# First query tiles of all batches computed ahead of everything else, in two units of 256 rows: a chunk-selecting attention with a feed-forward layer on one core

## The chip, the cores and the metric

The kernel runs on one core of a Trainium2 chip. Its time is the device time of one execution in microseconds (us); several executions are timed, and the median is compared. One further execution is profiled: its span runs from the first to the last instruction that the profiler saw on the core. The engines are PE (TensorE: matrix products and transposes), DVE (VectorE), ACT (ScalarE), POOL (GpSimd) and SP (SyncE, which only issues DMAs here). Each engine takes its instructions in order, and waits on semaphores for the others.

## What is computed

Attention over 4 batches, 8 heads, 768 positions and 64 channels, with a choice of key chunks per query; then a layer norm and a feed-forward layer with a residual:

```python
chunk = 32; nc = S // chunk; top_k = 6           # S = 768: 24 chunks
k_min, k_max = k_chunks.min(3), k_chunks.max(3)
ub = sum(maximum(q * k_min, q * k_max), -1)      # one bound per query and chunk
ub = where(pos // chunk >= chunk_index, ub, -1e9)
top_chunks = argsort(ub)[..., -top_k:]
scores = scale * q @ k.T                         # kept where chosen and causal
attn = softmax(where(sel & causal, scores, -1e9))
x = (attn @ v) heads side by side                # 4 x 768 x 512
xn = (x - mean) / sqrt(var + 1e-6) * g_ln
out = x + relu(xn @ w_ch1) @ w_ch2               # 512 -> 2048 -> 512
```

A query in the first 128 positions has at most four chunks in reach, which is fewer than six: it keeps all of them, and only the causal mask matters for it.

## The kernel before

Two heads of one batch form a pair; there are 16 pairs, numbered so that pairs 0 to 3 are batch 0, 4 to 7 batch 1, and so on. The 768 positions are six tiles of 128. The heads of a pair lie on the two halves of the 128 partitions.

**Loading.** `ldb` brings K or Q of a pair, 768 positions, in runs of 32 floats by four DMAs of SP, so that DVE's 32x32 block transpose (`turn`, L229) puts channels on partitions. Batch 0 is loaded differently (`ld`, runs of 64 floats, three tiles at a time) and is transposed by PE in float32 (L236). `ldv` brings V through POOL's queue, cast to half precision; `w1` and `w2` bring the two weight matrices through the same queue in four parts each, each behind a one-element copy that makes it wait for a pair's `kc`.

**Selection.** `kbound` (L288, L289) takes minimum and maximum of K per chunk; `kdiag` (POOL, L308 to L316) lays them out as operands. For pairs 4 to 15, `qhi` (L251 or L253), `qlo` (L256) and `qrel` (L262, L263) make half-precision parts of Q, `bounds` (L325) is 20 matmuls that give the bounds of tiles 1 to 5, and `select` adds the causal part (L351, L352), finds the eight largest of each row (L356) and compares (L357). For pairs 0 to 3 the same is done in float32 for half a sequence at a time (`qpos` on ACT, L338 on PE). The choice is transposed on PE (`maskt`, L366) and copied by DVE (`mring`) beside Q, so that masked scores come out of one matmul with 128 rows of contraction: 64 channels, and 24 rows of large negative numbers for chunks that were not chosen (`rrows`, from `RT`).

**Scores, values.** `smm(g, r, i)` (L419) fills one two-bank PSUM tile with up to four blocks of 128x128 per head; `sexp` (L427) takes the exponential on ACT, `diag` (L434) masks the diagonal blocks on POOL, `values` (L450) multiplies by V with a column of ones, `norm` (L464, L465) divides on DVE. r is 0 for query tiles 0 to 2, and 1 for tiles 3 to 5: six blocks and fifteen.

**Layer norm and feed-forward.** A unit is one half (b, r) of a batch, 384 rows; there are eight. `pstat` (L480) takes statistics per pair, `centre` (L489, L492) subtracts the mean and multiplies by the gain, `xt` (L509) is a transposing DMA of SP for each 128 rows, `m1` (L518) multiplies by two of the 16 column blocks of the first weight matrix into one PSUM tile, `relu` (L530 on ACT, L528 on DVE) writes half precision, `m2` (L543) adds four of 16 parts of the second product, and `fin` (L552, L557) scales, adds the residual and stores.

**Fillers.** `warm` and `busy` (L378, L117) are matmuls whose results nobody reads; they stand among the steps of batch 0.

**Order.** The text `ORDER` lists all steps; the loop under it calls them one after the other, and ties each instruction behind the one before it on the same engine. So every engine's queue is exactly that text, read from left to right. A number behind an @ selects another engine for a copy, or a number of fillers. What holds a step back is its data, and the buffers: PSUM has two two-bank tiles (`ps_m`: scores and first product) and four one-bank tiles (`ps_t`).

Of the kernel before, what the change touches and what calls it, by code (L numbers as in the profile page):

```python
# [19 lines left out]
def kernel(  # L20
# [10 lines left out]
    nc = tc.nc  # L31
# [8 lines left out]
    TR = NT // NR  # L40
# [19 lines left out]
    vap = ctx.enter_context(tc.tile_pool(name="vap", bufs=5))  # L60
# [3 lines left out]
    xp = ctx.enter_context(tc.tile_pool(name="xp", bufs=5))  # L64
    xcp = ctx.enter_context(tc.tile_pool(name="xcp", bufs=2))
    htp = ctx.enter_context(tc.tile_pool(name="htp", bufs=2))
# [8 lines left out]
    ident_b = const.tile([P, P], BF16, name="ident_b", tag="ident_b")  # L75
    causb = const.tile([P, NT - 1, 2, NCH], BF16, name="causb", tag="causb")
    causf = const.tile([P, NT - 1, 2, NCH], F32, name="causf", tag="causf")
    RT = const.tile([P, S], F16, name="RT", tag="RT")
    tiny = const.tile([1, 1], F32, name="tiny", tag="tiny")
    hsel = const.tile([P, 3, 2], F32, name="hsel", tag="hsel")  # L80
    mhalf = const.tile([P, TR], F32, name="mhalf", tag="mhalf")
    NK = 4
    QA = [ring.tile([P, S], F16, name=f"QA{i}", tag=f"QA{i}") for i in range(NK)]
    QB = [ring.tile([P, S], F16, name=f"QB{i}", tag=f"QB{i}") for i in range(NK)]
    KA = [ring.tile([P, S], F16, name=f"KA{i}", tag=f"KA{i}") for i in range(NK)]
    KB = [ring.tile([P, S], F16, name=f"KB{i}", tag=f"KB{i}") for i in range(NK)]
# [4 lines left out]
    MN = [ring.tile([P, NT - 1, P], F16, name=f"MN{i}", tag=f"MN{i}") for i in range(NM)]  # L91
# [7 lines left out]
    st = [dict() for _ in range(NG)]  # L99
    hf = {}  # L100
    x_tiles = {}

    other = [0]
    fill = {P: (8, 16, 32), 240: (4, 8, 16), 122: (8, 16, 32)}
# [7 lines left out]
    def busy(o):  # L114
        w = o.shape[1]
        for _ in range((0, *fill[w])[other[0]]):
            nc.tensor.matmul(o, ident_b, causb.rearrange("p s h c -> p (s h c)")[:, 0:w], start=True, stop=True)  # L117

    def consts():
        make_identity(nc, ident_f)
        rr = RT[0:64, :]
        nc.gpsimd.memset(rr, -NEGM)
        nc.gpsimd.affine_select(
            out=rr, in_=rr, compare_op=ALU.is_ge, fill=0.0,
            base=0, pattern=[[1, S]], channel_multiplier=-CH,
        )
        nc.gpsimd.affine_select(
            out=rr, in_=rr, compare_op=ALU.is_ge, fill=0.0,  # L130
            base=CH - 1, pattern=[[-1, S]], channel_multiplier=CH,
        )
        nc.gpsimd.memset(causb, 0.0)
        nc.gpsimd.affine_select(
            out=causb, in_=causb, compare_op=ALU.is_ge, fill=CAUSAL,
            base=P, pattern=[[P, NT - 1], [0, 2], [-CH, NCH]], channel_multiplier=1,
        )
        nc.vector.memset(hsel, 0.0)
        nc.scalar.activation(tiny, hsel[0:1, 0, 0:1], ACTF.Exp)
        nc.vector.memset(hsel[0:64, 0, 1:2], -KS)  # L140
        nc.vector.memset(hsel[64:P, 0, 0:1], -KS)
        nc.vector.memset(hsel[0:64, 1:3, 1:2], KS)
        nc.vector.memset(hsel[64:P, 1:3, 0:1], KS)
        for i in range(NM):
            nc.vector.memset(MN[i], 0.0)
        nc.vector.tensor_copy(ident_b, ident_f)
        nc.vector.tensor_copy(ident_h, ident_f)
        nc.scalar.dma_start(gall, moe_g_ln.rearrange("(o n) -> o n", o=1).to_broadcast([P, DM]))

    def late():  # L150
        nc.gpsimd.memset(mhalf, -0.5)
        nc.gpsimd.memset(causf, 0.0)
        nc.gpsimd.affine_select(
            out=causf, in_=causf, compare_op=ALU.is_ge, fill=CAUSAL,
            base=P, pattern=[[P, NT - 1], [0, 2], [-CH, NCH]], channel_multiplier=1,
        )

    def rinit(i):
        nc.vector.memset(QA[i][64:P, 0:P], 0.0)
        nc.vector.memset(QB[i][0:64, 0:P], 0.0)  # L160

    def rrows(i, r):
        c = slice(r * TR * P, (r + 1) * TR * P)
        eng = pick(nc.vector, nc.scalar)
        copy(eng, KA[i][64:P, c], RT[0:64, c])
        copy(eng, KB[i][0:64, c], RT[0:64, c])
# [3 lines left out]
    def w1(j, g):  # L170
        c = slice(j * HID // 4, (j + 1) * HID // 4)
        nc.gpsimd.tensor_copy(w1b[0:1, 0, c.start:c.start + 1], st[g]["kc"][0:1, 0, 0:1])
        nc.gpsimd.dma_start(w1b[:, :, c], w1_r[:, :, c])

    def w2(j, g):
        nc.gpsimd.tensor_copy(w2b[0:1, 4 * j, 0:1], st[g]["kc"][0:1, 0, NCH // 2:NCH // 2 + 1])
        nc.gpsimd.dma_start(w2b[:, 4 * j:4 * j + 4, :], w2_r[:, 4 * j:4 * j + 4, :])

    def ld(g, i):
        b, hp = divmod(g, HP)  # L180
        both = ldp.tile([P, 2, TR, 2, D], F32, name="raw", tag="raw")
        for e, (nm, src) in enumerate((("kn", k), ("qn", q))):
            t = st[g][nm, i] = both[:, e]
            for hh in range(2):
                nc.sync.dma_start(  # L185
                    t[:, :, hh], src[b, 2 * hp + hh, i * TR * P:(i + 1) * TR * P].rearrange("(t p) d -> p t d", p=P),
                )

    def ldb(g, nm):
        b, hp = divmod(g, HP)  # L190
        src = k if nm == "kn" else q
        t = st[g][nm] = ldp.tile([P, NCH, CH], F32, name=nm + "b", tag="raw")
        for u in range(4):
            nc.sync.dma_start(
                t[u * CH:(u + 1) * CH],
                src[b, 2 * hp + u // 2, :, u % 2 * CH:u % 2 * CH + CH].rearrange("(c j) d -> j c d", j=CH),
            )

    def ldv(g, i=None):
        b, hp = divmod(g, HP)  # L200
        if not i:
            st[g]["va"] = vap.tile([P, 2, NT, VW], F16, name="va", tag="va")
            nc.gpsimd.memset(st[g]["va"][:, :, :, D:D + 1], 1.0)
        va = st[g]["va"]
        if i is None:
            nc.gpsimd.dma_start(  # L206
                va[:, :, :, 0:D].rearrange("p h t d -> p (h t) d"),
                v[b, 2 * hp:2 * hp + 2].rearrange("h (t p) d -> p (h t) d", p=P),
            )
            return  # L210
        a, z = i * TR, i * TR + TR
        for hh in range(2):
            nc.gpsimd.dma_start(  # L213
                va[:, hh, a:z, 0:D], v[b, 2 * hp + hh, a * P:z * P].rearrange("(t p) d -> p t d", p=P),
            )
# [3 lines left out]
    def span(g, i):  # L219
        return (i * TR, i * TR + TR) if g < HP else (0, NT)  # L220

    def chosen(g, i):
        a, z = span(g, i)
        return max(a, 1), z, z * P // CH

    def turn(g, nm, i=None):
        if g >= HP:
            t = prp.tile([P, S], F32, name=nm + "T", tag="T")
            nc.vector.transpose(t, st[g][nm].rearrange("p c e -> p (c e)"))  # L229
            st[g][nm, i] = t  # L230
            return
        pst = ps_t.tile([P, 512], F32, name="tr", tag="one")
        src = st[g][nm, i]
        busy(pst[:, TR * P:512])
        for t in range(TR):
            nc.tensor.transpose(pst[:, t * P:(t + 1) * P], src[:, t], ident_f)  # L236
        st[g][nm, i] = pst[:, 0:TR * P]

    def qpos(g, i):
        qt = st[g]["qn", i]  # L240
        u = P if i == 0 else 0
        for nm, sign in (("q32", -1.0), ("r32", 1.0)):
            st[g][nm] = prp.tile([P, TR * P], F32, name=nm, tag=nm)
            nc.scalar.activation(st[g][nm][:, u:], qt[:, u:], ACTF.Relu, scale=sign)

    def qhi(g):
        for nm in ("q", "r"):
            t2 = prp.tile([P, 2, S], F16, name=nm + "2", tag=nm + "32")
            st[g][nm + "h"], st[g][nm + "l"] = t2[:, 0], t2[:, 1]
        if other[0]:  # L250
            nc.vector.tensor_scalar(st[g]["qh"], st[g]["qn", None], QS, None, op0=ALU.mult)  # L251
        else:
            nc.scalar.activation(st[g]["qh"], st[g]["qn", None], ACTF.Copy, scale=QS)  # L253

    def qlo(g):
        nc.vector.scalar_tensor_tensor(  # L256
            st[g]["ql"][:, P:], st[g]["qn", None][:, P:], QS, st[g]["qh"][:, P:], op0=ALU.mult, op1=ALU.subtract,
        )

    def qrel(g):  # L260
        qh, ql, rh, rl = (st[g][nm][:, P:] for nm in ("qh", "ql", "rh", "rl"))
# [3 lines left out]
    def qring(g, i=None):  # L265
        if HP <= g < HP + 2:
            eng = pick(nc.vector, nc.scalar, nc.gpsimd)
# [3 lines left out]
        if i is None:  # L271
            nc.sync.dma_start(QA[g % NK][0:64, :], st[g]["qh"][0:64, :])
            nc.sync.dma_start(QB[g % NK][64:P, :], st[g]["qh"][64:P, :])
            return
        qt = st[g]["qn", i]
        a, z = span(g, i)
        nc.scalar.activation(QA[g % NK][0:64, a * P:z * P], qt[0:64, :], ACTF.Copy, scale=QS)
        nc.scalar.activation(QB[g % NK][64:P, a * P:z * P], qt[64:P, :], ACTF.Copy, scale=QS)

    def kbound(g, i=None):  # L280
        kt = st[g]["kn", i]
        a, z = span(g, i)
        n = slice(a * P // CH, z * P // CH)
        view = kt.rearrange("p (c e) -> p c e", e=CH)
        if not i:
# [411 lines left out]
```

The softmax here doesn't subtract the row's maximum and nothing guards it: scores larger than these inputs give would overflow.

## Time and profile before

| | us |
|---|---|
| median of 13 runs | 280.4 (278.81 to 284.83) |
| profiled execution, its time | 279.92 |
| its span | 278.2 |
| ACT busy in the span | 177.8 |
| POOL busy | 99.8 |
| DMA, mean over the span | 115 GB/s |

The profile page gives busy time per engine and, in 40 slices of 6.96 us, its share in tenths. The clock that the throttle granted to TensorE is full in all of them. An engine's busy time counts overlapping instructions once, so that it is below the sum of the durations: DVE has 632 instructions. The "idle before" of a group is the time for which its engine stood still just ahead of it, with what it waited for. The chain of waits begins at the last instruction and goes back to what released it; most of it is PE's feed-forward matmuls (L543 29%, L518 26%), and its last wait for another engine's data of more than two microseconds is a transposing DMA that lands at 128.6.

### The profile page before, as it was taken

To read this page: it belongs to the slowest core of one execution; us is meant where nothing else is said; L and a number is where in the kernel's file an instruction comes from. 1 tells how busy PE (TensorE), PEld (TensorE's weight loads), DVE (VectorE), ACT (ScalarE), POOL (GpSimd) and SP (SyncE) were. 2 spreads that over 40 slices of the span, in tenths; PEclk is the share of its full clock that TensorE was granted. 3 is DMA by queue.
4 is the path that set the end of the run, shared out by engine and by line. 5 is a ranking of instruction groups with operands and counts; after the bars stand their busy time and mean duration, and the time that the engine had idled before them with its cause. 6 is when DMAs were issued, how large, how long until landed. Compare 5 with 4: busy or idle time off the path is not lost.

```text
span 278.2 us, 6816 instructions
## 1 busy us (share of the span) xinstructions
PE 268.7 (97%) x2643; PEld 180.1 (65%) x2643; DVE 215.4 (77%) x632; ACT 177.8 (64%) x237; POOL 99.8 (36%) x170
## 2 busy tenths in 40 slices
PE   7989998989999999999999999999999999999994
PEld 3989896677557775666667765566666655555541
DVE  6889999899999999998899989897876665021212
ACT  3878997889957767667665787577777332413310
POOL 8615565956472043734152804320164000100100
PEclk9999999999999999999999999999999999999999
DMA  6999999999999895999514899564021012210202
GB/s 163 203 178 170 180 159 175 164 129 185 152 174 140 143 197 99 105 171 187 61 41 97 133 136 122 69 185 83 0 68 40 38 45 70 76 40 38 75 5 113
DMA packets 135745, 32.05 MB, mean 115 GB/s; under 512 B 127008, under 2 KB 132640, under 8 KB 135712
## 3 DMA queue, kind: packets, MB, share of 16 engines
q1 hardware_dynamic: 106320, 24.00, 44.8%
q0 software_dynamic: 29248, 7.34, 28.8%
q8 instruction: 21, 0.34, 0.5%
q10 hardware_dynamic: 144, 0.26, 0.3%
q14 instruction: 12, 0.10, 0.1%
HBM read 27.53 MB, written 6.29 MB: 122 GB/s over the span
## 4 chain that ended last, share of the span: by engine, by line
PE 77%; DVE 8%; DMA 6%; SPq 4%; ACT 1%; issue 1%; DVEq 0%; ACTq 0%
PE yp L543 29%; PE mm L518 26%; PE mm L419 11%; PE sm L450 6%; SPq L185 4%; DMA xT<-xc 4%; PE ub L325 3%; DMA raw<-in_q_dram 2%; DVE xc L492 1%; DVE bst L480 1%; ACT pt L427 1%; PE trh L366 1%; DVE x L465 1%; PE ub L338 1%; DVE ot L552 1%
## 5 line engine op out<-in xcount | busy, mean ns | idle before, releaser
L427 ACT ACTIVATE pt<-mm 128x1024 f16<-128x1024 f32 (+2 forms) x96 | 84.4, 916 | 21.3 <-PE mm L419 19.2
L543 PE MATMUL yp<-w2b,hT 128*128 128x512 f16 (+2 forms) x400 | 93.0, 370 | 0.0
L518 PE MATMUL mm<-xT,w1b 128*128 128x384 f16 x512 | 88.3, 326 | 1.5 <-DMA xT<-xc 1.5
L530 ACT ACTIVATE hT<-mm 128x768 f16<-128x768 f32 x61 | 49.2, 809 | 61.6 <-PE mm L518 61.4
L518 PEld LDWEIGHTS <-w1b 128*128 128x128 f16 x512 | 49.4, 98 | 35.1 <-issue 1.7
L543 PEld LDWEIGHTS <-hT 128*128 128x128 f16 x400 | 37.3, 98 | 33.3
L434 POOL TENSOR_SCALAR_AFFINE_SELECT pt<-pt 128x768 f16<-128x768 f16 x32 | 30.4, 955 | 48.9 <-ACT pt L427 48.7
L552 DVE SCALAR_TENSOR_TENSOR ot<-yp,rstd,x 128x512 f32<-128x512 f32 (+2 forms) x25 | 17.9, 720 | 31.2 <-PE yp L543 17.7
L419 PE MATMUL mm<-QA,KA 128*128 128x128 f16 (+2 forms) x224 | 34.0, 245 | 0.9 <-ACT pt L427 0.7
L419 PE MATMUL mm<-QB,KB 128*128 128x128 f16 (+2 forms) x224 | 34.0, 246 | 0.0
L503 POOL TENSOR_TENSOR rstd<-ve,mhalf 128x3 f32<-128x3 f32 x8 | 7.0, 880 | 54.2 <-DVE ve L500 54.2
L450 PEld LDWEIGHTS <-pt 128*128 128x128 f16 x672 | 23.9, 98 | 1.8
L450 PE MATMUL sm<-va,pt 128*128 128x65 f16 x672 | 25.0, 193 | 0.0
L419 PEld LDWEIGHTS <-KA 128*128 128x128 f16 x224 | 18.1, 98 | 9.7 <-issue 1.4
L308 POOL TENSOR_TENSOR kc<-kc 128x24 f32<-128x24 f32 x12 | 4.8, 401 | 50.6 <-DVE kc L289 50.5
L419 PEld LDWEIGHTS <-KB 128*128 128x128 f16 x224 | 17.9, 98 | 3.8 <-issue 0.4
L480 DVE BATCH_NORM_STATS2 bst<-x 128x6 f32<-128x128 f32 x96 | 20.1, 275 | 0.0
L465 DVE TENSOR_TENSOR x<-sm,rden 128x384 f32<-128x384 f32 x32 | 17.8, 558 | 1.1
L492 DVE SCALAR_TENSOR_TENSOR xc<-x,mv,gall 128x512 f16<-128x512 f32 x24 | 17.6, 786 | 1.3 <-DMA xT<-xc 1.3
L213 POOL DMA_DIRECT2D va<-in_v_dram x16 | 12.7, 794 | 0.0
L206 POOL DMA_DIRECT2D va<-in_v_dram x12 | 12.7, 1057 | 0.0
L356 DVE MAX8 m<-ubm 128x8 f32<-128x24 f32 x120 | 11.4, 170 | 0.4
(100 smaller groups left out, 349.1 us busy)
## 6 DMA issues: line engine op xcount, KB each, us to landing
out_dram<-ot SPq DMA_DIRECT2D x23, 256.0 KB, 2.1
qnb<-in_q_dram SPq DMA_DIRECT2D x48, 96.0 KB, 3.4
knb<-in_k_dram SPq DMA_DIRECT2D x48, 96.0 KB, 3.1
va<-in_v_dram POOLq DMA_DIRECT2D x12, 192.0 KB, 6.0
w1b<-in_moe_w_ch_dram POOLq DMA_DIRECT2D x4, 512.0 KB, 6.8
w2b<-in_moe_w_ch_dram POOLq DMA_DIRECT2D x4, 512.0 KB, 6.8
raw<-in_k_dram SPq DMA_DIRECT2D x16, 96.0 KB, 3.7
raw<-in_q_dram SPq DMA_DIRECT2D x16, 96.0 KB, 3.5
```

The lines of the kernel that those rows point to most:

```text
L206: nc.gpsimd.dma_start(va[:, :, :, 0:D].rearrange("p h t d -> p (h t) d"), v[b, 2 * hp:2 * hp + 2].rearrange("h (t p) d -> p (h t) d", p=P),)
L419: nc.tensor.matmul(sc[:, hh, o:o + w * P], ks[:, t * P:(t + 1) * P], qs[:, s * P:(s + w) * P], start=True, stop=True,)
L427: nc.scalar.activation(st[g]["pt", r][:, 4 * i:4 * i + o].rearrange("p n h x -> p h n x"), st[g]["sc", r, i][:, :, 0:o * P].rearrange("p h ...
L434: nc.gpsimd.affine_select(out=dv, in_=dv, compare_op=ALU.is_ge, fill=0.0, base=0, pattern=[[0, 2 * TR], [1, P]], channel_multiplier=-1,)
L450: nc.tensor.matmul(pv[:, hh, s2, :], pt[:, where[t, s], hh, :], va[:, hh, t, 0:D + 1], start=(t == 0), stop=(t == s),)
L465: nc.vector.tensor_tensor(xh(b, r)[:, :, 2 * hp:2 * hp + 2, :].rearrange("p s h d -> p h s d"), pv[:, :, :, 0:D], rden.to_broadcast([P, 2, ...
L480: nc.vector.bn_stats(half(b, r)["st"][:, i, hp], xh(b, r)[:, i, 2 * hp:2 * hp + 2].rearrange("p h d -> p (h d)"),)
L492: nc.vector.scalar_tensor_tensor(h["xc"][:, i, :], xs, h["mv"][:, i, 0:1], gall, op0=ALU.subtract, op1=ALU.mult,)
L518: nc.tensor.matmul(hp_[:, i, 0:TR * P], w1b[:, kt, (m + i) * P:(m + i + 1) * P], h["xT"][:, kt], start=(kt == 0), stop=(kt == KT1 - 1),)
L530: nc.scalar.activation(h["hT"][:, m:m + 2], h["hp", m][:, :, 0:TR * P], ACTF.Relu, scale=HS)
L543: nc.tensor.matmul(h["yp", i][:, cs], h["hT"][:, kt, i * P:(i + 1) * P], w2b[:, kt, cs], start=(kt == 0), stop=(kt == KT2 - 1),)
L552: nc.vector.scalar_tensor_tensor(ot[:, cs], h["yp", i][:, cs], h["rstd"][:, i:i + 1], xh(b, r)[:, i].rearrange("p h d -> p (h d)")[:, cs], ...
```

## The change

**The first query tile.** Rows 0 to 127 of all batches leave the pairs. New steps, each for a whole batch (eight heads), do them without any selection: `lda` (K and Q, one DMA each of 256 KB, K on SP and Q on ACT's queue), `ldva`, `turna` (four float32 transposes on PE into one bank), `kbounda` (chunk minima and maxima of the first four chunks of four pairs at once), `kcopya`, `qcopya`, `smma` (eight 128x128 blocks with 64 rows of contraction), `sexpa`, `diaga`, `valuesa`, `norma`, `pstata`. The first tile's K and V stay in SBUF (`KA0`, `KB0`, `va0`) for the later tiles of their batch; `rows0` fills the mask rows of `KA0` and `KB0` by two copies of 64x2048 on POOL.

**Units.** The first tiles of batches 0 and 1 are unit 0, those of batches 2 and 3 are unit 1; each batch then has a unit of tiles 1 and 2 (256 rows) and one of tiles 3 to 5 (384 rows). That makes ten units instead of eight. In 256-row units `m1` fills its PSUM tile with four column blocks instead of two, and `relu` takes 1024 columns instead of 768. `hT` is kept in four parts per unit.

**All pairs alike.** K and Q of a pair are 640 positions; batch 0 takes the path of the others (`ldb`, DVE transposes, half-precision bounds). `ld`, `qpos`, the float32 bounds, the PE transposes of batch 0, `warm` and `busy` are gone. Weight loads lose their one-element copies. The order has no @: `kcopy`, `qhi` and `relu` are always ACT's, `mring` DVE's, `qring` SP's two DMAs.

**Order.** The whole text is new. It begins with the first tiles, runs units 0 and 1 through the feed-forward layer between the pairs of batch 0, and ends with the unit of tiles 3 to 5 of batch 3.

```diff
-    TR = NT // NR
+    LO, HI = (1, 3), (3, NT)
+    NQ = NT - 1
+    SQ = NQ * P
...
-    vap = ctx.enter_context(tc.tile_pool(name="vap", bufs=5))
+    vap = ctx.enter_context(tc.tile_pool(name="vap", bufs=4))
...
-    xp = ctx.enter_context(tc.tile_pool(name="xp", bufs=5))
+    xp = ctx.enter_context(tc.tile_pool(name="xp", bufs=3))
...
-    htp = ctx.enter_context(tc.tile_pool(name="htp", bufs=2))
+    htp = ctx.enter_context(tc.tile_pool(name="htp", bufs=8))
...
-    def busy(o):
-        w = o.shape[1]
-        for _ in range((0, *fill[w])[other[0]]):
-            nc.tensor.matmul(o, ident_b, causb.rearrange("p s h c -> p (s h c)")[:, 0:w], start=True, stop=True)
...
+    def rows0():
+        eng = pick(nc.gpsimd, nc.vector)
+        eng.tensor_copy(KA0[64:P], RT[0:64, 0:P].unsqueeze(1).to_broadcast([64, NG, P]))
+        eng.tensor_copy(KB0[0:64], RT[0:64, 0:P].unsqueeze(1).to_broadcast([64, NG, P]))
...
-    def w1(j, g):
+    def w1(j):
         c = slice(j * HID // 4, (j + 1) * HID // 4)
-        nc.gpsimd.tensor_copy(w1b[0:1, 0, c.start:c.start + 1], st[g]["kc"][0:1, 0, 0:1])
         nc.gpsimd.dma_start(w1b[:, :, c], w1_r[:, :, c])
...
+    def lda(b, nm):
+        if "raw" not in sa[b]:
+            sa[b]["raw"] = xp.tile([P, 2, H, D], F32, name="rawa", tag="x2" if b == B - 1 else "x3")
+        t = sa[b][nm] = sa[b]["raw"][:, 0 if nm == "kn" else 1]
+        eng = nc.sync if (nm == "kn") != bool(other[0]) else nc.scalar
+        eng.dma_start(t, (k if nm == "kn" else q)[b, :, 0:P].rearrange("h p d -> p h d"))
...
+    def smma(b):
+        sc = sa[b]["sc"] = ps_m.tile([P, 2, 512], F32, name="mm", tag="mm")
+        for hp in range(HP):
+            for hh in range(2):
+                c = slice(hh * D, hh * D + D)
+                nc.tensor.matmul(
+                    sc[:, hh, hp * P:(hp + 1) * P], (KB0 if hh else KA0)[c, b * HP + hp], sa[b]["qa"][c, hp],
+                    start=True, stop=True,
+                )
...
+    def per(u):
+        return 4 if nt(u) == 2 else 2
...
-        for i in range(2):
+        for i in range(per(u)):
+            o = (i % (per(u) // 2)) * w
             for kt in range(KT1):
                 nc.tensor.matmul(
-                    hp_[:, i, 0:TR * P], w1b[:, kt, (m + i) * P:(m + i + 1) * P],
+                    hp_[:, i // (per(u) // 2), o:o + w], w1b[:, kt, (m + i) * P:(m + i + 1) * P],
                     h["xT"][:, kt], start=(kt == 0), stop=(kt == KT1 - 1),
                 )
...
+    END = (9, 2)
     ORDER = """
+        lda.1.qn ident lda.0.kn lda.1.kn ldb.0.qn half_ ones turna.0.kn masks lda.0.qn ldb.0.kn turna.1.kn
+        turna.1.qn lda.2.qn ldb.1.kn ldva.0 lda.3.kn rows turna.0.qn small kcopya.0 lda.3.qn idh rrows.3 rrows.0
+        rrows.2 lda.2.kn rrows.1 ldb.1.qn rows0 qcopya.0 caus kbounda.1 smma.0 turna.2.qn turn.0.qn kbounda.0
+        sexpa.0 diaga.0 turn.0.kn qhi.0 qcopya.1 kbound.0 valuesa.0 qlo.0 kcopya.1 qrel.0 turn.1.kn smma.1
+        qring.0 kdiag.0 bounds.0 sexpa.1 turna.2.kn norma.0 ldva.1 select.0 turna.3.qn qcopya.2 ldva.2
+        turna.3.kn kcopy.0 ldb.2.qn gain diaga.1 turn.1.qn w1.3 pstata.0 kcopya.2 maskt.0 mring.0 smm.0.1.1
+        ldva.3 kbound.1 kcopya.3 qcopya.3 qhi.1 kdiag.1 valuesa.1 sexp.0.1.1 smma.2 qlo.1 norma.1 sexpa.2
+        smm.0.1.0 smma.3 qrel.1 pstata.1 centre.0 diaga.2 sexp.0.1.0 valuesa.2 bounds.1 sexpa.3 smm.0.0.0 xt.0.0
...
+        sexp.11.1.2 kdiag.13 diag.11.1 turn.14.qn pstat.8.1 turn.15.kn diag.11.0 relu.5.12 bounds.12 qring.12
...
```

## The prediction

> **What bounds the kernel now.** I read the busy tenths of the page first, then VectorE's busy time in four stretches, the time line where two queues meet, the chain of waits, and the groups by form.
>
> ```profile
> PE 268.7 (97%) x2643; PEld 180.1 (65%) x2643; DVE 215.4 (77%) x632; ACT 177.8 (64%) x237; POOL 99.8 (36%) x170
> ...
> PE   7989998989999999999999999999999999999994
> ...
> DVE  6889999899999999998899989897876665021212
> ```
>
> TensorE looks full from the second slice on and VectorE for the first two thirds. Neither alone sets 278.2 us: both queues are in order and feed each other. The stretches say how full VectorE is (columns: stretch, its length, busy time and instructions, clock, DMA share, GB/s):
>
> ```profile
> 0.00:20.00 20.00, 15.69 (x63) 1.00 1.08 182
> 20.00:76.00 56.00, 53.79 (x168) 1.00 1.23 165
> 76.00:120.00 44.00, 42.26 (x121) 1.00 1.01 145
> 120.00:175.00 55.00, 50.32 (x144) 1.00 0.90 118
> ```
>
> It idles 4.3 us in the opening, then only 3.95 us in the 100 us from 20 to 120. TensorE's real pace is read from dense pieces of the chain, start to start:
>
> ```profile
> 176.36 6.50 PE mm L518 x40
> ...
> 267.47 6.92 PE yp L543 x32
> ```
>
> A 384-column matmul takes 0.1625 us, a 512-column one 0.216; the 326 and 379 ns of the groups hold pipeline time. In the same way I read 0.0545 per 128 columns of scores, 0.0303 for a 65-column value matmul, 0.85 for the 20 bound matmuls of a pair. The last matmul ends at 274.4, so the **tail** is 3.8.
>
> The meeting point is the bounds of pair 6, `bounds.6`:
>
> ```profile
> 73.74 0.82 DVE L263 SCALAR_TENSOR_TENSOR r<-q 128x640 f16<-128x640 f16 x1
> ...
> 74.99 0.22 PE L325 MATMUL ub<-BH,q 128*128 128x96 f16 x2
> ```
>
> VectorE ends its last input at 74.56 and TensorE starts it within half a microsecond. All TensorE steps from there on in the order sum to 199.6 at those paces (88 groups of L543 at 0.86, 56 of L518 at 1.30, scores 24.5, values 15.2, bounds 8.5, transposes 2.8). 74.8 + 199.6 + 3.8 = 278.2: the span. So **VectorE sets the time up to about 75 us, TensorE after it**. I use this formula for the new order: VectorE's work ahead of a point, plus its idle time, plus TensorE's work behind it, plus the tail; the largest over all points counts. VectorE's work is the sum over instructions of mean durations (a MAX8 at its pace of 0.095) times 0.926, since neighbours overlap: all steps before sum to 232.5 where the page has 215.4. For `bounds.6` that gives 69.2; the stretches have 69.5 by 76.
>
> **The change, part by part.**
>
> ```profile
> L263 DVE SCALAR_TENSOR_TENSOR r<-q 128x640 f16<-128x640 f16 x12 | 11.7, 971 | 0.0
> L229 DVE STREAM_TRANSPOSE knT<-knb 128x768 f32<-128x768 f32 x12 | 11.6, 963 | 0.0
> L356 DVE MAX8 m<-ubm 128x8 f32<-128x24 f32 x120 | 11.4, 170 | 0.4
> L288 DVE TENSOR_REDUCE kc<-knT 128x24 f32<-128x768 f32 x12 | 11.3, 938 | 0.0
> L338 PE MATMUL ub<-BD,r 128*128 128x48 f32 x24 | 4.6, 275 | 0.0
> L236 PE MATMUL tr<-ident_f,raw 128*128 128x128 f32 x48 | 7.4, 278 | 1.2 <-DMA raw<-in_q_dram 0.7 <-ACT QB L112 0.5
> L117 PE MATMUL tr<-causb,ident_b 128*128 128x128 bf16 x80 | 5.1, 219 | 0.1
> L528 DVE TENSOR_SCALAR hT<-mm 128x768 f16<-128x768 f32 x3 | 2.9, 955 | 8.5 <-PE mm L518 8.5
> ```
>
> *TensorE.* Scores cover the same 21 blocks per head, values the same 672 matmuls: nothing. The second product (L543) is unchanged. Of the 512 first-product matmuls half the columns become 256 wide, 384 of them beside 256 of 384. Pairs of 256-column matmuls in the score rows start 0.22 apart:
>
> ```profile
> 32.68 0.38 PE L419 MATMUL mm<-QA,KA 128*128 128x256 f16 x2
> 32.90 0.38 PE L419 MATMUL mm<-QB,KB 128*128 128x256 f16 x2
> 33.12 0.38 PE L236 MATMUL tr<-ident_f,raw 128*128 128x128 f32 x2
> ```
>
> At 0.11 each, 42.2 + 41.6 against 83.2: +0.6. Float32 bounds of the first four pairs go (80 instructions of L338 at 0.11 = -8.8, eight openings -0.7), four more pairs of half-precision bounds come (+3.4). Float32 transposes: 48 to 32 at 0.107, -1.7. The fillers go: 144 of L117 at 0.055 to 0.10 (-11) and 11 opening matmuls (-4.4). In all 267.4 falls to 245.0. But the fillers run where TensorE had nothing else to do, and all of this lies ahead of `bounds.6`; its removal costs and saves **nothing by itself** as long as VectorE sets that part.
>
> *VectorE.* Added by batch 0 becoming like the others: transposes 24 x 0.966 to 32 x 0.80 (+2.5), L256/L262/L263 for four more pairs (+9.0), selection 32.8 to 16 x 2.21 (+2.6), first-tile minima and maxima bring L288/L289 to 31.0 (-0.4), normalisation and statistics +0.6. Dropped: three ReLUs (-2.9), four qhi (-2.2), copies and row setup (-6.9). That is +2.3, times 0.926: 215.4 becomes 217.5. **The work is the same; its place is not**: batch 0 now has all of it, and first-tile work of all four batches comes ahead too.
>
> *ScalarE* stays at 178 (56 ReLUs of 0.81 or, by the 1024-wide exponentials, 1.02, against 61 of 0.81); cover for it is its 36% idle time. *GpSimd* gains about 15 (four more pairs of bound operands at 1.6, four masks, and two 64x2048 copies, 4.4 by L112's 0.82 for 768) on 64% idle; the copies stand ahead of the first mask, and delay it by at most 4.4. *SP* takes six more pairs' query copies, 12 issues at 0.5, ahead of transposes and loads.
>
> *The new meeting point.* Going through the order step by step, VectorE is ahead of TensorE by nearly the same from 33 to 190 us; the largest sum is at `bounds.12`. VectorE ahead of it: 28 transposes 22.4, minima and maxima 22.0, L256 11.8, L262 and L263 19.5, 12 selections 26.5, mask copies 11.8, normalisation 13.5, statistics 8.8, six centrings 12.5, ten outputs 7.2, first-tile steps 11.8, opening and rest 6.7: 174.5, times 0.926 = 161.6. TensorE behind it: first product 8 x 1.75 + 20 x 1.30 = 40.0, 53 groups of L543 at 0.86 = 45.6, scores 10.9, values 7.0, bounds 3.4, transposes 1.1: 108.0. With 0.3 of handover and the tail, 161.6 + 0.3 + 108.0 + 3.8 = **273.7 with a VectorE that never idles**. In the kernel before, the same sum is 273.0, and the span 278.2 has the idle time on top.
>
> *The unknown is VectorE's idle time by then.* The point moves from 75 to about 172 us, so the queue has 100 us more in which small waits count: 4.3 for the opening plus 3.95% of 152 = 6.0, in all 10.3. Bounds: the opening alone, 4.3 (no later wait), and 17 (opening 8, later 6%; the stretch from 120 to 175 has 8.5%, much of it behind a full TensorE). I take 10.3, since the stretch from 20 to 120 is the one in which VectorE led. 273.7 + 10.3 = **284.0 span**.
>
> *A rule against the change.* The first weight loads of the opening are 0.43 us apart:
>
> ```profile
> 3.11 0.15 PEld L378 LDWEIGHTS <-MN 128*128 128x128 f16 x1 [0.28 <-issue]
> 3.53 0.15 PEld L378 LDWEIGHTS <-MN 128*128 128x128 f16 x1 [0.28 <-issue]
> ```
>
> that is, twice the 0.216 of the same 512 columns later, though the granted clock shows 1.00. Without fillers the 10.3 us of TensorE work ahead of the first feed-forward matmul may run at this pace; 20.6 still fits under VectorE's 25.3 + 4.3 + 5.2 for the transposing DMA. Only handovers grow: four times 0.24 of values, twice 0.85 + 0.28 of bounds and mask, 3.2 at most; I take 0. The Trainium skill (TensorE: Matmul & The Clock Gate, section Part 1: The HAM clock gate) says that the array falls back to half rate after an idle window of some 3.4 us and needs about as much sustained work to recover. By that rule those 3.2 would be paid in full and the span be 287.2.
>
> **From span to time.** The profiled execution took 279.92, 1.7 above its span; the median 280.4 is 0.5 above that. 284.0 + 2.2 = **286.2, say 286**. Half a percent, 1.4 us, is what this measurement can tell from no change: 279.0 to 281.8 is "same".
>
> **Rivals.** *Faster:* VectorE's lead disappears because units 0 and 1 give TensorE 28 us of work early (2 x 64 matmuls of 0.11, 64 of 0.216) that needs only 33 us of VectorE's, so nothing on VectorE waits for TensorE. For: no wait for a filler is left. Price: 1.5 in the opening, 1% later, span 276.7, time 278.9. It decides once VectorE's idle time by `bounds.12` is under 3.1; the opening alone had 4.3. 13%. *Same:* waits at half the old rate or work 2% lighter, about 280.5. 17%. *The opening starves for data:* the DMA share is above 1 there, and 10.6 MB moved in the first nine slices, 62.6 us, 169 GB/s. Ahead of `select.4` the new order asks for first tiles 2.6 MB, K and Q 3.9, V 0.5, weights 4.2, transposes and query copies 1.3: 12.5 MB, 74 us, where VectorE would come at 68. 6 us more: span 290, time 292. Against: in the old opening VectorE was still 96% busy under a DMA share of 1.23. 20%. The forecast itself: 50%.
>
> **Numbers.** 286; range 279 to 293, from the faster rival's edge to just above the starved opening; the forecast's own is 282 to 290. Faster 13%, same 17%, slower 70%.
>
> **What would show it.** VectorE busy 217, TensorE 245 plus pipeline time; `bounds.12` at about 172, right behind the product of pair 12 that L263 makes now; TensorE's last idle time near there and not near 45. If `bounds.12` starts before 165, or TensorE is dense from 100 on, I am wrong towards faster; if the first centring comes after 38 or weights release TensorE, towards the starved opening.

## The result, and the profile after

The changed kernel takes 301.0 us, the median of 11 runs (298.75 to 306.56), against 280.0 before (48 runs): a ratio of 1.073, interval 1.070 to 1.0755. The prediction was 286 with a range to 293: the sign was right, the size was not. The profiled execution shown here took 304.5, some one per cent more than the median; its span is 302.8. Medians here and below are of all runs, while ratios and intervals compare fast runs alone (within 1.5% of the kernel's fastest), to which the profiled executions of the changed kernel and of e9 don't belong.

The busy tenths of the page, 40 slices of 7.57 us each; the rows are TensorE, VectorE, the granted clock and the mean share of the DMA engines:

```profile
PE 262.1 (87%) x2624; PEld 181.8 (60%) x2624; DVE 218.7 (72%) x615; ACT 175.7 (58%) x218; POOL 109.0 (36%) x185
...
PE   1636667977899699799989989999999998999995
...
DVE  5889996855699998889999998999874254500212
...
PEclk9998779989599899999999999999999999999999
DMA  9999999999739987698994761405591012200122
```

Before, TensorE was at 9 from the second slice on and VectorE for two thirds of the span. Now TensorE has 1 to 7 in the first seven slices, as intended, but VectorE has no steady 9 there either: it falls to 6, 8, 5, 5 and 6 from slice 7 to 11, about 45 to 83 us, while the DMA row stands at 9 without a break for the first ten slices. By itself that row tells nothing of a cause, since before it stood at 9 for twelve slices from the second on, with VectorE 95% busy:

```profile
DMA  6999999999999895999514899564021012210202
```

VectorE's work is what the prediction said (218.7 against 217); it is spread over a longer time. VectorE in the same four stretches as before (columns: stretch, length, busy time and instructions, clock, DMA share, GB/s):

```profile
0.00:20.00 20.00, 14.62 (x26) 1.00 1.26 166
20.00:76.00 56.00, 43.27 (x116) 0.88 1.28 163
76.00:120.00 44.00, 39.33 (x117) 0.89 0.91 128
120.00:175.00 55.00, 51.76 (x158) 1.00 0.86 127
```

From 20 to 76 us VectorE works 43.3 us, where it worked 53.8 before; after 120 it is fuller than before. So the loss lies in the first hundred microseconds. The waits of VectorE by 100 us (what it waited for; us in total, times, longest):

```profile
DVE knT L287 <- DMA knb<-in_k_dram: 5.9, 3, 3.4
DVE qnT L287 <- DMA qnb<-in_q_dram: 5.6, 4, 3.5
DVE ubt L355 <- PE ub L344: 3.8, 3, 2.1
DVE KA L114 <- POOL RT L131: 2.5, 1, 2.5
```

The loads of K and Q are the largest, 11.5 us; before, the same transposes had no idle time ahead of them. The bounds come third; a pair whose K or Q lands late has late bounds too. The meeting point that the prediction named, `bounds.12`, in the time lines of VectorE and TensorE:

```profile
188.38 0.82 DVE L307 SCALAR_TENSOR_TENSOR r<-q 128x640 f16<-128x640 f16 x1
...
190.33 0.22 PE L344 MATMUL ub<-BH,q 128*128 128x96 f16 x2
```

Its last input from VectorE is ready at 189.2, TensorE finishes a step of eight first-product matmuls that it began at 189.0, and comes to it at 190.3, not at 172. From there TensorE needs 108.7 us and the tail 3.8: 190.3 + 108.7 + 3.8 = 302.8, where the prediction had 108.3 and 3.8. Everything that is lost is lost ahead of the meeting point.

### The profile page after: what moved, and what is told of

Read it like the earlier page. It is cut to its first block, busy times and chain, and to the rows that moved or that the text cites. A ratio compares the mean times of both kernels' runs of the same rounds, so it can differ in the third digit from the quotient of the medians.

```text
span 302.8 us, 6793 instructions
## 1 busy us (share of the span) xinstructions
PE 262.1 (87%) x2624; PEld 181.8 (60%) x2624; DVE 218.7 (72%) x615; ACT 175.7 (58%) x218; POOL 109.0 (36%) x185
## 4 chain that ended last, share of the span: by engine, by line
PE 60%; DMA 16%; DVE 14%; ACT 3%; SPq 3%; issue 2%; DVEq 0%; ACTq 0%
PE mm L538 24%; PE yp L567 21%; PE mm L416 7%; DMA xT<-xc 6%; PE sm L450 4%; DMA qnb<-in_q_dram 4%; DMA knb<-in_k_dram 3%; PE ub L344 3%; SPq L199 2%; DMA rawa<-in_q_dram 2%; DMA gall<-in_moe_g_ln_dram 1%; DVE q L300 1%; DVE qnT L287 1%; DVE xc L509 1%; PE trh L368 1%
## 5 line engine op out<-in xcount | busy, mean ns | idle before, releaser
L538 PE MATMUL mm<-xT,w1b 128*128 128x256 f16 (+1 forms) x640 | 93.0, 301 | 11.3 <-DMA xT<-xc 10.0
L538 PEld LDWEIGHTS <-w1b 128*128 128x128 f16 x640 | 63.2, 100 | 36.3 <-issue 12.0
L554 ACT ACTIVATE hT<-mm 128x768 f16<-128x768 f32 (+1 forms) x56 | 50.4, 900 | 54.3 <-PE mm L538 54.1
L435 POOL TENSOR_SCALAR_AFFINE_SELECT pt<-pt 128x512 f16<-128x512 f16 (+1 forms) x32 | 26.1, 822 | 58.4 <-ACT pt L427 58.4
L209 POOL DMA_DIRECT2D va<-in_v_dram x32 | 28.4, 892 | 0.5 <-issue 0.4
L331 POOL TENSOR_TENSOR kcs<-kcs 128x24 f32<-128x24 f32 x16 | 4.8, 301 | 50.0 <-DVE kcs L321 49.0
L520 POOL TENSOR_TENSOR rstd<-ve,mhalf 128x2 f32<-128x2 f32 (+1 forms) x10 | 7.8, 783 | 36.3 <-DVE ve L517 36.1
L287 DVE STREAM_TRANSPOSE qnT<-qnb 128x640 f32<-128x640 f32 x16 | 13.4, 836 | 6.2 <-DMA qnb<-in_q_dram 5.6
L287 DVE STREAM_TRANSPOSE knT<-knb 128x640 f32<-128x640 f32 x16 | 13.3, 836 | 6.0 <-DMA knb<-in_k_dram 5.9
L344 PE MATMUL ub<-BH,q 128*128 128x96 f16 (+4 forms) x160 | 13.7, 209 | 3.6 <-POOL BH L337 3.6
```

The costliest lines, as they stand in the source:

```text
L209: nc.gpsimd.dma_start(va[:, hh, :, 0:D], v[b, 2 * hp + hh, P:S].rearrange("(t p) d -> p t d", p=P))
L344: nc.tensor.matmul(ub[:, s, :, :, 0:w], st[g][nm][:, s * P:(s + 1) * P], BH[g % NB][:, arr, :, :, 0:w], start=(e == 0), stop=(e == 3),)
L435: nc.gpsimd.affine_select(out=dv, in_=dv, compare_op=ALU.is_ge, fill=0.0, base=0, pattern=[[0, 2 * (z - a)], [1, P]], channel_multiplier=-1,)
L538: nc.tensor.matmul(hp_[:, i // (per(u) // 2), o:o + w], w1b[:, kt, (m + i) * P:(m + i + 1) * P], h["xT"][:, kt], start=(kt == 0), stop=(kt ...
L554: nc.scalar.activation(o, i, ACTF.Relu, scale=HS)
```

## The experiments

Two theories stood against each other. **Data:** ahead of pair 4 the new order asks for more loads than the DMA engines bring by then, and VectorE waits. **Clock:** TensorE, sparse and without fillers, runs at a lower granted clock (0.81 to 0.91 between 20 and 80 us), and its handovers grow. A third, smaller one was the copies on GpSimd in the opening. The ratio is to the kernel before on the same chip; "point" is the start of `bounds.12`, "work" VectorE's busy time by then in the profiled execution, "idle" the difference.

| | median us | ratio, interval | point | work | idle |
|---|---|---|---|---|---|
| predicted | 286 | | 172 | 161.6 | 10.3 |
| changed kernel | 301.01 | 1.073 (1.070 to 1.0755) | 190.3 | 162.9 | 27.4 |
| e1 fillers | 303.69 | 1.080 (1.073 to 1.087) | 189.2 | 163.6 | 25.6 |
| e2 quarter weights | 292.11 | 1.040 (1.031 to 1.048) | 179.0 | 162.9 | 16.1 |
| e3 both | 300.45 | 1.069 (1.061 to 1.077) | 185.5 | 162.6 | 22.9 |
| e4 before, no fillers | 281.83 | 1.004 (0.999 to 1.008) | | | |
| e5 row copies on VectorE | 301.07 | 1.069 (1.057 to 1.081) | 184.8 | 161.1 | 23.7 |
| e6 one load for K and Q | 291.59 | 1.036 (1.028 to 1.044) | 175.1 | 161.7 | 13.4 |
| e7 e2, e5 and e6 | 289.38 | 1.027 (1.020 to 1.034) | 173.3 | 159.7 | 13.6 |
| e8 before, quarter weights | 279.39 | 0.994 (0.990 to 0.997) | | | |
| e9 long runs | 291.84 | 1.031 (1.022 to 1.040) | 177.5 | 161.6 | 15.9 |
| e10 Q on ACT's queue | 300.24 | 1.068 (1.061 to 1.074) | 185.4 | 163.1 | 22.3 |
| e11 second weights later | 299.71 | 1.066 (1.060 to 1.073) | 185.4 | 163.0 | 22.4 |
| e12 before, long runs | 280.17 | 0.999 (0.994 to 1.004) | | | |

Work hardly moves; idle does, and the point and the time with it. e10 and e11 have the changed kernel's time, and their profiled executions lie nearer to the median than that of the changed kernel: 22 is taken as its usual idle time.

### e1_fillers: is it the clock?

```diff
+    def busy(o):
+        for _ in range(other[0]):
+            nc.tensor.matmul(o, ident_h, ident_h, start=True, stop=True)
...
-        rrows.2 lda.2.kn rrows.1 ldb.1.qn rows0 qcopya.0 caus kbounda.1 smma.0 turna.2.qn turn.0.qn kbounda.0
+        rrows.2 lda.2.kn rrows.1 ldb.1.qn rows0 qcopya.0 caus kbounda.1 smma.0@8 turna.2.qn turn.0.qn kbounda.0
```

Fillers stand ahead of 28 steps of the opening, and eight `warm` at its start.

> The changed kernel with fillers again: eight opening matmuls on zeros, and 4 to 60 matmuls of the identity on itself ahead of 28 steps of the first 80 us in which TensorE waited. Clock theory (the fillers kept the array at full pace; without them it runs part of 20 to 120 us at half pace): granted clock 1.00, 299 falls to 287 to 292. Data theory (loads land late, VectorE waits for them): 298 to 301. Order theory (neither; the handovers of the new order cost it): 298 to 301.

Measured: 303.7, no gain, and above all three forecasts. The granted clock did rise; the stretches of TensorE in this kernel:

```profile
20.00:40.00 20.00, 14.45 (x236) 1.00 1.27 137
40.00:60.00 20.00, 17.27 (x198) 1.00 1.33 164
60.00:80.00 20.00, 20.00 (x312) 1.00 1.42 181
```

The clock is 1.00 where it was 0.83, 0.91 and 0.81, but VectorE's busy time by 80 us is 62.1, against 61.5 without fillers (63.6 in e10, below, which has none either). A full clock made by fillers brings VectorE nothing. As the fillers also stand in TensorE's queue, this run alone doesn't clear the clock. Two kernels without fillers do more: e9 is faster than the changed kernel with a clock of 0.82 between 20 and 76 us, where the changed kernel has 0.88, and in e7, whose loads are cut, the clock is 1.00 over the first 100 us. The low clock goes with the waiting; what it costs beside the loads is not separated.

### e2_quarter_weights, e3_fillers_quarter_weights: the data theory, and the clock again

```diff
-        nc.gpsimd.dma_start(w1b[:, :, c], w1_r[:, :, c])
+        nc.gpsimd.dma_start(w1b[:, 0, c], w1_r[:, 0, c])
...
-        nc.gpsimd.dma_start(w2b[:, 4 * j:4 * j + 4, :], w2_r[:, 4 * j:4 * j + 4, :])
+        nc.gpsimd.dma_start(w2b[:, 4 * j, :], w2_r[:, 4 * j, :])
```

The matmuls read the quarter that is there. e3 has the fillers of e1 as well.

> The changed kernel with a quarter of the two weight matrices loaded (each slab read four times in its place; the products use the wrong weights, the same instructions run). 6.3 MB less to read in the first 75 us. Data theory: the waits of L287 for qnb and knb go, 299 falls to 283 to 290. Clock theory: 296 to 300, since TensorE still idles in the opening. Order theory: 298 to 301.

> Both at once: quarter of the weights and the fillers. If the two causes are separate, the gains of e1 and e2 add; if a cold array only fills time that the loads cost anyway, this equals e2. My sum without either cause was 284 to 286.

Measured: 292.1 and 300.5. Without three quarters of the weight loads the point comes at 179.0 and the time falls by 9: the data theory holds in kind, though not in size. It had 283 to 290, and the waits of L287 for K and Q by 100 us fall from 11.5 to 4.3 us instead of going. With most of them gone, the fillers show what they cost: 8 us, since now they stand in front of matmuls whose inputs are ready. VectorE's waits for TensorE by 100 us are 8.6 us in e3 and 0.5 in e2.

### e4_before_no_fillers, e8_before_quarter_weights: the same edits on the kernel before

```diff
-    fill = {P: (8, 16, 32), 240: (4, 8, 16), 122: (8, 16, 32)}
+    fill = {P: (0, 0, 0), 240: (0, 0, 0), 122: (0, 0, 0)}
```

e4 also drops `warm`; e8 has the edit of e2 in the kernel before.

> The kernel before without its 144 fillers and 11 opening matmuls, everything else as it was. Clock theory: 280 rises to 284 to 290, granted clock under 1 in the first 60 us. Data theory and order theory: 279 to 281. My prediction counted the fillers at nothing.

> Control: the kernel before with a quarter of the weights loaded (wrong products, same instructions). Data theory: its opening was fed in time, so 277 to 280; if weights hold up any kernel of this kind alike, it gains as much as e2 did, 7 to 9 us.

Measured: 281.8 and 279.4. The fillers were worth nothing that this comparison can tell (0.4%, interval -0.1 to 0.8%), though the granted clock fell to 0.74 between 20 and 40 us; 281.8 lies between the two forecasts. A quarter of the weights gains 0.6% (0.3 to 1.0%) there, against 3% in the changed kernel. The kernel before was fed in time, but for that 0.6%.

### e5_rows0_vector: the copies on GpSimd

```diff
-        rrows.2 lda.2.kn rrows.1 ldb.1.qn rows0 qcopya.0 caus kbounda.1 smma.0 turna.2.qn turn.0.qn kbounda.0
+        rrows.2 lda.2.kn rrows.1 ldb.1.qn rows0@1 qcopya.0 caus kbounda.1 smma.0 turna.2.qn turn.0.qn kbounda.0
```

> The changed kernel with the two 64x2048 copies of rows0 on VectorE instead of GpSimd. Shared-memory theory (two 64x640 copies of VectorE took 1.9 us instead of 0.32 while GpSimd made these copies, 3.2 us lost): minus 3.2 plus two copies of about 1 us, and the first minima and maxima start 1 us earlier: 299 to 300, 1 us at most gained. If loads set the opening, 0: VectorE only waits longer for qnb.

Measured: 301.1, no gain, although VectorE's own copies in the opening become 3.2 us shorter (the last section shows why) and the two large ones add only 1.4. What is saved becomes waiting: from 0 to 20 us VectorE's busy time falls from 14.6 to 13.0.

### e6_one_load_for_k_and_q, e7_all_three: fewer loads of the pairs

```diff
         src = k if nm == "kn" else q
-        t = st[g][nm] = ldp.tile([P, NCH - NC4, CH], F32, name=nm + "b", tag="raw")
+        t = st[g][nm] = st[g]["raw1"] = ldp.tile([P, NCH - NC4, CH], F32, name=nm + "b", tag="raw")
```

The second of the two loads of a pair is left out, and its transpose reads the first one's tile. e7 takes e2, e5 and e6 together.

> The changed kernel with one load per pair instead of two (K and Q of a pair are both taken from whichever is named first; same instructions otherwise, 5.2 MB less in 128-byte runs). Data theory: the waits for qnb and knb (11.5 us) shrink; with the weights still in, 288 to 294. If only the weights crowd the queues: 297 to 300.

> Quarter of the weights, one load for K and Q, rows0 on VectorE. If waits for data in the opening are all that my sum missed, VectorE reaches the bounds of pair 12 at 172 and the time is 284 to 287. If the new order loses more in its own handovers, it stays above 289.

Measured: 291.6 and 289.4. Leaving out eight times 768 KB of weights or sixteen times 320 KB of K and Q (as read from memory) brings the same, and both together little more, which suggests that each is enough to end most of the same queueing. In e7 VectorE's stretch after the opening is nearly what it was before the change:

```profile
20.00:76.00 56.00, 52.33 (x150) 1.00 0.74 89
```

The point comes at 173.3, where the prediction had 172, and the time is still 2.7% above the kernel before: 289.4 is just past the "stays above 289" that stood for the new order's own handovers, not the 284 to 287 of waits for data alone. By this comparison two things add up: some 12 us of a starved opening (from a ratio of 1.073 to 1.027), and some 8 us that stay when it is fed.

### e9_long_runs, e12_before_long_runs: bytes, or pieces?

```diff
-                t[u * CH:(u + 1) * CH],
-                src[b, 2 * hp + u // 2, P:S, u % 2 * CH:u % 2 * CH + CH].rearrange("(c j) d -> j c d", j=CH),
+                t[u * CH:(u + 1) * CH].rearrange("p c e -> p (c e)"),
+                src[b, 2 * hp + u // 2, P + u % 2 * 320:P + u % 2 * 320 + 320].rearrange("(j y) d -> j (y d)", j=CH),
```

> The changed kernel with the same DMAs, bytes and targets for K and Q of rows 128 to 767, but read from memory in runs of 2,560 bytes instead of 128 (each partition gets 10 whole positions in a row), so that positions and channels are mixed up in what the pairs compute. If the opening is late because of the bytes of all loads together, the time stays within 1% of the changed kernel (297 to 304 us) and bounds.12 starts between 184 and 191. If it is late because of the short runs, that is, because a transfer of 80 KB in 128-byte pieces holds the DMA engines far longer than its bytes need, the time falls by as much as in the kernel that loads one of K and Q: about 290 us (287 to 293), bounds.12 at 175 or before, and VectorE's idle time between 40 and 80 falls from 11.8 us to under 5.

> The kernel before with the K and Q loads of its pairs 4 to 15 read in runs of 3,072 bytes instead of 128, so that positions and channels are mixed up in what these pairs compute; batch 0 keeps its runs of 256 bytes. If short runs cost time only where VectorE leads and waits for its loads, the kernel before has next to nothing to gain, because its first 24 loads of this kind stand behind an opening that was fed in time: 278.5 to 281 us, ratio 0.992 to 1.0. If the pieces cost every kernel that uses them, the time falls by 1.5% or more, below 276.5 us.

Measured: 291.8 and 280.2. With every byte loaded, the time falls by 8.4 us against e10 on the same chip (by 10 by the ratios, 1.068 to 1.031), as much as by leaving out half the loads of K and Q. Bytes alone don't explain it: short pieces do, by the time for which they hold the DMA engines. Two of its numbers missed: the point came at 177.5, not by 175, and VectorE idled 7.8 us between 40 and 80, not under 5; 3.6 us of it is one wait for `bounds.2`, which TensorE reached at 53.8, behind first-product matmuls that had waited 2.7 us for a transposing DMA. SP's queue of hardware DMAs on the page of the changed kernel (packets, MB, share of 16 engines):

```profile
q1 hardware_dynamic: 107344, 23.61, 43.4%
```

and on that of e9:

```profile
q1 hardware_dynamic: 29520, 23.61, 32.0%
```

The bytes are equal. 0.434 x 16 x 302.8 = 2103 us of one engine's time against 0.320 x 16 x 291.2 = 1491: 612 us for 77,824 packets, 7.9 ns for each. The ten loads of pairs 0 to 4 have 25,600 such packets, 202 us of one engine, by estimate 12.6 us of all sixteen; packets' times overlap (the share is 1.28 in the first 100 us of e10), so that is rather too high than too low. In the kernel before the same edit takes 0.448 x 16 x 278.2 - 0.354 x 16 x 278.6 = 416 us of engine time away and the time doesn't move. The likely reason: there batch 0 came in runs of 256 bytes, and the short runs stood behind an opening that already had TensorE full.

The Trainium skill (DMA: Bandwidth & Descriptors, section Why small descriptors are slow (HBM only)) gives a fixed overhead of some three cycles for each packet beside one cycle per 32 bytes. By it, an estimate, 3 of 7 cycles of a 128-byte packet would be overhead; the runs agree in kind, with the 7.9 and 5.9 ns (416 us over 70,656 packets) that a short packet costs beyond its bytes.

### e10_q_on_scalar_queue, e11_w2_later: the queue, and the collision

```diff
-            nc.sync.dma_start(
+            (nc.scalar if nm == "qn" and 0 < g < 4 else nc.sync).dma_start(
```

e11 moves two steps of the order: `w2.2` to just ahead of `m2.1.0.1`, `w2.3` to just ahead of `rstd.1`.

> The changed kernel with the Q loads of pairs 1 to 3 issued by ScalarE instead of SP: the same bytes in the same pieces, but SP has 12 issues fewer ahead of the K loads and the transposing DMAs. If the DMA engines themselves are full, nothing is gained: 298 to 304 us. If SP's queue was the narrow place (four issues of it took 7 us twice), the K loads that were issued at 57.7 and 66.5 us come 3 to 6 us earlier, and the time falls to 293 to 297 us.

> The changed kernel with the last two of the four loads of the second weight matrix issued some 8 to 12 us later, just ahead of their use, so that they do not stand with the K and Q loads of pairs 3 and 4. Nothing is left out. If only the sum of bytes counts, the wait moves and the time stays within 1% (298 to 304 us). If it is the collision around 60 to 75 us, VectorE's idle time between 60 and 80 falls from 7.9 to 3 to 5 us and the time by 3 to 5 us, to about 297 us.

Both were tried because of SP's time line in the changed kernel:

```profile
57.68 7.41 SPq L199 DMA_DIRECT2D knb<-in_k_dram  x4
...
66.53 7.17 SPq L199 DMA_DIRECT2D knb<-in_k_dram  x4
```

Four issues take 7 us; in e9, with the long runs, the load at that place takes 2.2:

```profile
55.03 2.24 SPq L199 DMA_DIRECT2D knb<-in_k_dram  x4
```

Measured: 300.2 and 299.7, no change beyond the intervals, where 293 to 297 and about 297 would have spoken for the queue and for the collision. The mark of the queue failed too: e10's K loads were issued at 58.2 and 67.2, not 3 to 6 us earlier, and with fewer issues in its queue SP still took 7.0 and 6.5 us for four. So SP's queue is not the narrow place; the last section shows that the same issues are short once the engines are freer. In e11 VectorE's idle time between 60 and 80 did fall, from 7.9 to 3.2, as that theory had it; but e10, whose weights were not moved, has 2.6 there, and both begin `bounds.12` at 185.4. A later load moves the wait and doesn't remove it.

## Why the prediction was off

**Right, or nearly.** In the execution of e10, whose time is nearest to the changed kernel's median, 163.1 work + 22.3 idle + 109.8 TensorE + 3.8 tail = 299.0, its span. The work was predicted as 161.6, TensorE's part with its handover as 108.3. One reading behind the latter was off: the 20 bound matmuls of a pair take 0.69 us (`bounds.6` from 74.99 to 75.68, `bounds.12` of the changed kernel from 190.33 to 191.02), not 0.85, which takes 1.6 from the 199.6 and 0.6 from the 108.0, so that the exact 278.2 was partly luck. The removal of the fillers "costs and saves nothing by itself": e4 shows -0.2 to +2.2 us for it in the kernel before, e1 and e3 that new ones bring nothing or cost; there is no sign there that the 3.2 us of the clock rule were paid. The copies on GpSimd are hidden in the time, since e5 gains nothing; that they lengthen VectorE's own copies by 3.2 us the prediction did not have.

**Not shown by that sum** is that VectorE leads up to `bounds.12`. The sum closes whatever leads, because idle is what the work leaves of the point. Parts of the chain of waits of the changed kernel:

```profile
62.69 10.54 DMA knb<-in_k_dram
73.42 0.86 DVE knT L287
...
98.95 3.69 DMA xT<-xc
102.78 7.07 PE mm L538 x48
```

Up to 102.8 it runs mostly over loads, VectorE and transposing DMAs, and from there to the point mostly over TensorE. Between 100 us and the point VectorE's waits in e10 are for ScalarE and TensorE, none for a load, and at `bounds.6` in the kernel before, too, TensorE was still at work when VectorE's input was ready. In e7, with most loads out of the way, the chain stays with VectorE most of the way to 160. So in the changed kernel the loads do their harm before some 100 us, and from there on neither engine alone is shown to lead.

**The step that failed** is "The unknown is VectorE's idle time by then": 4.3 for the opening plus 3.95%, 10.3 in all, and 17 at most. It is about 22, so the term was taken at half its size: 12 of the 15 us that are missing between 284.0 and 299.0; 1.5 are work and 1.5 TensorE's part. What stood in its place were waits for K and Q in the first 100 us, 10.3 of the 16.9 us that VectorE idles there in e10. The 3.95% came from a stretch whose loads had been ordered early, partly in longer runs. For the 16.9 us the prediction's terms give 4.3 + 0.0395 x 80 = 7.5, and for another 5.4 from 100 to 185 they give 3.4. Even fed (e7) it idles 11.1 by 100.

**The rival that should have carried it** was there with 20%: the opening starves for data. Its mechanism is shown, by e2, e6 and e9. Its price of 6 us was too low: some 12 us go with the loads (e7). It had the data for pair 4 at 74 us, by bytes at the 169 GB/s of the old opening; the new one moved 10.9 MB in its first nine slices (68.1 us at a mean of 161 GB/s), and 12.5 MB at that rate take 78. The selection of pair 4 began at 82.7 (78.6 in e10), and with the same bytes in long runs (e9) at 73.7: the pieces belong into the price. The 68 us of a fed VectorE were early as well; with lighter loads it still comes there at 70.3 (e7). "Against: in the old opening VectorE was still 96% busy under a DMA share of 1.23" was no evidence: with a share of 1.28 in the same stretch the changed kernel's VectorE is 77% busy. The share says that the engines are full, not whether what they bring is needed next.

**The marks it named** didn't tell the cases apart. The first centring came at 32.6, not after 38, and the weights did not show as what released TensorE; by both the opening would have counted as fed. The weights did their harm one step aside, by standing on the same engines as K and Q. Waits of the transposes for `knb` and `qnb`, and the point at 190, were the sign.

**The sign** is partly luck, since the larger part of the 21 us came with the loads, a cause that had 20%. The forecast's own reason was the step "the point moves from 75 to about 172 us, so the queue has 100 us more in which small waits count". e7 supports it: with most loads out of the way it lands at 289.4, 3 above the forecast, and still slower than before. e7 loads less than the real kernel and keeps waits of its own (3.4 us for one Q, 2.5 for `RT`), so what the order alone costs is not settled more closely than some 8 us, and its cause stays open.

None of the changed kernel's versions beats the kernel before. Loading batch 0 in longer runs again, which needs its transposes elsewhere, was not tried.

## What to carry to other kernels

When independent work is brought forward to fill an idle engine, add up the loads that are due ahead of each early step, in pieces as well as in bytes, and at the rate that pieces of this size had; the busy share of the old opening says nothing about the new one. An idle rate belongs to the stretch it was read from: before it is carried to another, see what that stretch had already been given. A low granted clock beside a starved engine can be a sign of waiting, as here; try whether it goes when the engine is fed before filling it.

## What the runs showed of the hardware

**GpSimd slows VectorE's half-precision copies.** The time lines of GpSimd and VectorE in the changed kernel:

```profile
5.22 2.04 POOL L172 COPY KA<-RT 64x2048 f16<-64x2048 f16 x1
...
5.53 1.91 DVE L114 COPY KB<-RT 64x640 f16<-64x640 f16 x1
7.45 1.93 DVE L114 COPY KA<-RT 64x640 f16<-64x640 f16 x1
```

and VectorE in e5, where it makes the large copies itself a little later:

```profile
6.13 0.32 DVE L114 COPY KA<-RT 64x640 f16<-64x640 f16 x1
...
8.14 0.69 DVE L172 COPY KA<-RT 64x2048 f16<-64x2048 f16 x1
```

A copy of 0.32 us takes 1.91 beside GpSimd's, and GpSimd needs 2.04 for what VectorE does in 0.69. Both long copies of VectorE end 0.2 us after one of GpSimd's two does (7.26 and 9.21). The Trainium skill (GPSIMD Engine Reference, section 1. Specifications) says that the two share their interfaces to SBUF, with contention where VectorE runs in a two-port mode or reads two inputs from SBUF; the numbers agree with such contention, though no trace here shows the mode.

**An issue can wait for the engines.** Four K loads took SP 7.41 us to issue under a DMA share of 1.3, and 2.24 with long runs. The query copies of the next pair stand right behind them in SP's queue and were issued at 65.2 us, right after the fourth K load. The short runs alone don't make an issue long: in the same execution, under a share of 0.60 between 160 and 173 us, four of the same kind take

```profile
169.28 2.05 SPq L199 DMA_DIRECT2D knb<-in_k_dram  x4
```
